# Chunk 0 of a delta-rule attention with an MLP: key scores first, query scores inside the substitution, w_in in its own row order

## The chip, the cores and the metric

The kernel runs on one core of a Trainium2 chip. The metric is the device time of one execution in microseconds; the time before is the median of three runs. Engines are named as in the profile: PE (matmuls; PEld are its weight loads), DVE, ACT, POOL, and SP, whose queue issues every DMA of this kernel.

## The reference

Two parts follow one another. The first is a delta-rule linear attention over B = 4 batches, H = 8 heads, S = 768 steps and D = 48; the second is an MLP with SiLU over 3072 rows, 384 wide, 2048 hidden.

```python
k_n = k / (np.linalg.norm(k, axis=-1, keepdims=True) + 1e-06)
state = np.zeros((B, H, D, D))
for t in range(S):
    kt, vt, bt = k_n[:, :, t], v[:, :, t], beta[:, :, t, None]
    y[:, :, t] = np.einsum('bhd,bhde->bhe', q[:, :, t], state)
    v_old = np.einsum('bhde,bhd->bhe', state, kt)
    state = state + bt[..., None] * np.einsum('bhd,bhe->bhde', kt, vt - v_old)
x = y.transpose(0, 2, 1, 3).reshape(B * S, H * D)
h = x @ w_in
out = (h * (1.0 / (1.0 + np.exp(-h)))) @ w_out
```

The weights come as 64-bit floats, so every piece of w_in and w_out is loaded raw (two words a number) and narrowed to 32 bits on the chip.

## The kernel before

**Chunks and units.** The 768 steps are cut into six chunks of 128; a unit is one batch in one chunk, with all eight heads. In a chunk, a triangular system is solved for each head: scores of keys with keys (j = 0) and of keys with queries (j = 1) are formed, the diagonal 32x32 blocks are inverted, and solve() combines them.

**Steps of a chunk.** squares() and norms() make the step sizes g (L338) from the keys alone. turn() transposes keys (its first part) and queries (its second) on PE (L376), and ACT copies them into kq (L383, L381). score() multiplies them (L399): with one weight load of the keys it takes keys and queries in one matmul of 256 columns, and ACT (L409) and DVE (L415) scale the results by g and mask them with `above` into ap. block_out() writes the diagonal blocks to DRAM by four DMAs a unit (L443), block_in() fetches them again as rows of g (L451), 32 partitions a unit. invert() is the substitution: 30 dependent steps on DVE, each a product (L477) and a sum (L481); at its end x goes out as up and its transposed copy g (ACT L485, DVE L486) as low (L492), and 12 DMAs move them into xe and xi (L502). solve() begins with merges (L551, four in all; first py, then px), goes on with seven steps k that pipeline inner, across, add, keep, old, update and new over the four units, and leaves the result in xT.

**The MLP.** feed_forward() multiplies xT by w_in (hidden(), L719), applies SiLU on ACT (L729), and multiplies by w_out (project(), L742, for chunk 0; combine(), L813, with fewer products, from chunk 1 on). It is a generator, `pieces`, that is advanced between the steps of the next chunk's preparation, substitution and solve, and so fills PE.

**Order.** pin() keeps the instructions of each compute engine in the order in which the program writes them; in_line() does the same for all DMAs on SP. Nothing overtakes on an engine. busy() is a dummy matmul (pw, L276; two instructions each) that keeps PE occupied where it has no work; one group of 20 of them stands before solve(0) and waits for a late step of the substitution.

**Weights.** w_in comes in eight pieces of 256 columns. Its rows are permuted (ROWS): partitions 0 to 47 and 64 to 111 hold the heads 0 to 5, and what is left of a 64-row half holds thirds of heads 6 and 7. So each piece is four DMAs (L215), over 48, 16, 48 and 16 partitions. narrow() takes three steps a piece: ACT L165 and L170, DVE L167, L173 and L177, and POOL L181. fill(n) advances n such steps. Pieces are kept in the spare places of other tiles until they are narrowed.

**From a unit's result to xT.** Rows of xT have the order of w_in's rows. In chunk 0, whose state is zero, a copy of heads 6 and 7 in thirds (`third`, L605) is used as weights by new() (L648), so that the sums come out in order, and one copy makes xT (L659). In the chunks 1 to 5 new() copies heads 6 and 7 to `last` (L662), the other six straight to xT (L665, on ACT and DVE), and six DMAs of 16 rows move the thirds (L669). load_q() for the next chunk follows on SP (L128).

Loads before the first score: beta, k of four units, q of four units, and two pieces of w_in.

Of the kernel before, what the change touches and what calls it, by code (L numbers as in the profile page):

```python
# [21 lines left out]
def kernel(  # L22
# [22 lines left out]
    nc = tc.nc  # L45
# [97 lines left out]
    for load_one in (load_k, load_q):  # L143
        for i in range(B):
            load_one(i)
    w_in = const.tile([P, NKT, DFF], FP32, name="w_in")
    HFF = NFF // 2


    ROWS = [  # L150
        (at, lambda a, e=e, n=n: (2 * a + e) * D if n == D else (6 + e) * D + a * (W - D), n)
        for e in range(2)
        for at, n in ((W * e, D), (W * e + D, W - D))
    ]
# [44 lines left out]
    def fetch_w_in(i):  # L199
# [7 lines left out]
        for at, row, rows in ROWS:  # L207
            step = row(1) - row(0)
            src = moe_w_in[row(0) : row(0) + rows, i * WF : (i + 1) * WF].bitcast(U32)
            pitch = src.ap[0][0]  # L210
            src = bass.AP(
                tensor=src.tensor, offset=src.offset,
                ap=[[pitch, rows], [pitch * step, NKT], [1, 2 * WF]],
            )
            in_line(nc.sync.dma_start(out=raw[at : at + rows], in_=src))  # L215
        raws[i] = raw.rearrange("p a (f j) -> p a f j", j=2)
# [7 lines left out]
    sums_of_w = [const.tile([P, NFF // 2, HM], FP32, name=f"sums_of_w{i}") for i in range(3)]  # L224

    def narrow_w_in(i):
        return narrow(w_in[:, :, i * WF : (i + 1) * WF], raws.pop(i))
# [3 lines left out]
    def fetch_w_out(i):  # L231
        if i in (0, 1, 5):
            raw = room(1, min(i, 1))
        elif i in (4, 7):
            raw = sums_of_w[2 if i == 4 else 0][:].rearrange("p f m -> p (f m)").bitcast(U32)
# [10 lines left out]
        raws[i] = raw.rearrange("p a (f j) -> p a f j", j=2)  # L246

    def narrow_w_out(i):
        at = 2 * i % HFF
        return narrow(w_outs[2 * i // HFF][:, at : at + 2, :], raws.pop(i))  # L250
# [45 lines left out]
    def squares(c):  # L296

        sums[c] = small.tile([P, BH], FP32, name="ss", bufs=1)[:]
        for b in range(B):
            if c == 1:  # L300
                sq = packed(zbufs[b])
            else:
                if b % HB == 0:
                    two = work.tile([P, HB, H, D], FP32, name="sq", tag="xg"[b // HB], bufs=1)
# [121 lines left out]

    def block_out(i, u):
# [19 lines left out]
    def block_in(i):  # L447
        b, c = units[i]
        there, g, _ = blocks[c]
        rows = slice(T * b, T * (b + 1))  # L450
        in_line(nc.sync.dma_start(out=g[rows], in_=there[b].rearrange("h j s t -> (h j) s t")))  # L451

    def invert(c):
# [41 lines left out]
        if c == 0:  # L495
            xe = sums_of_w[1][:].rearrange("p f m -> p (f m)")[:, 0 : BH * T]
# [16 lines left out]
    xTs, xes = {}, {}  # L513

    def solve(c, us):
# [6 lines left out]
        pzs, pys, third = {}, {}, {}  # L522
# [5 lines left out]

# [372 lines left out]
    for t in turning:  # L901
        next(t)
# [188 lines left out]
```

## Time and profile before

| what | value |
|---|---|
| median of 3 runs | 772.79 us (772.77 to 773.8) |
| the profiled execution, its own time | 770.21 us |
| its span | 768.5 us |
| mean granted clock | 0.977 |
| PE busy | 730.4 us (95%) |
| DVE busy | 411.8 us (54%) |
| ACT busy | 233.3 us (30%) |
| POOL busy | 83.6 us (11%) |
| moved by DMA | 50.93 MB in 155067 packets |

Times inside the profile are counted from the start of the span. A row of the timeline gives start, length, engine, line and operation, what is written and read, the shapes, how many, and in brackets the idle time before with what ended it. A row of the busy times by stretch gives the stretch, its length, the busy time of PE, PEld, DVE, ACT and POOL with the number of instructions, the granted share of the PE clock, the mean busy share of the DMA engines, and the GB/s that they moved. In the chain of waits a row is start, length and what the chain passed through; "issue" is time in which an engine waited for nothing that the profile shows.

### The profile page before, as it was taken

The page shows a single profiled execution, that of the slowest core. Times are in us where ns is not written, and L with a number is a line of the kernel's source. Part 1 is how long each engine was busy: PE and PEld are TensorE (multiplying, and loading weights), DVE is VectorE, ACT ScalarE, POOL GpSimd, SP SyncE. Part 2 cuts the span into 40 slices and gives each one's busy share as a digit, 9 for nine tenths or more (in the row PEclk, how much of TensorE's full clock was granted, in tenths as well). Part 3 has the DMA queues.
Part 4 walks back from the last instruction along what each step waited for, and adds up shares of the span by engine and source line. Part 5 has one row for each costly group of instructions (what it writes and reads, how often), then busy time and mean ns, then how long its engine had stood idle before and what let it go on. Part 6 is the DMA issues. An engine that isn't in the chain of part 4 may idle for free.

```text
span 768.5 us, 16585 instructions
## 1 busy us (share of the span) xinstructions
PE 730.4 (95%) x6806; PEld 630.0 (82%) x6806; DVE 411.8 (54%) x1050; ACT 233.3 (30%) x512; POOL 83.6 (11%) x95
## 2 busy tenths in 40 slices
PE   7549799899999999999999999999999999999997
PEld 5336587478777999997999997999998999999987
DVE  4886678892336672445672445672445682221212
ACT  4524465311325212315212315212315212312020
POOL 4005246300003000002000002000002000000000
PEclk8859999999999999999999999999999999999999
DMA  9798847212025213034113044113043013010000
GB/s 164 116 167 162 172 146 194 52 66 42 13 54 106 42 48 70 6 77 101 33 49 69 5 77 96 38 49 70 5 77 77 15 49 70 5 30 0 21 1 21
DMA packets 155067, 50.93 MB, mean 66 GB/s; under 512 B 142544, under 2 KB 147536, under 8 KB 154992
## 3 DMA queue, kind: packets, MB, share of 16 engines
q1 hardware_dynamic: 154992, 49.87, 31.1%
q8 instruction: 54, 0.88, 0.5%
q14 instruction: 21, 0.17, 0.1%
HBM read 34.70 MB, written 14.16 MB: 64 GB/s over the span
## 4 chain that ended last, share of the span: by engine, by line
PE 88%; DVE 4%; DMA 3%; SPq 2%; issue 1%; ACT 1%; POOL 1%; ACTq 0%; DVEq 0%
PE phid L719 31%; PE px L813 14%; PE py L813 11%; PE pa L399 6%; PE pz L583 4%; PE pt L376 3%; PE po L742 3%; PE pw L276 3%; PE pyc L642 3%; PE pyc L614 2%; PE ph L567 2%; DMA z<-in_q_dram 2%; PE px L551 2%; PE py L551 2%; PE pu L625 2%; DVE x L481 1%
## 5 line engine op out<-in xcount | busy, mean ns | idle before, releaser
L719 PE MATMUL phid<-xT,w_in 128*128 128x256 f32 x1152 | 260.7, 382 | 2.2 <-ACT gT L729 1.6
L719 PEld LDWEIGHTS phid<-xT,w_in 128*128 128x128 f32 x1152 | 214.8, 190 | 37.2 <-issue 6.3
L729 ACT ACTIVATE gT<-phid 128x512 f32<-128x512 f32 x96 | 57.3, 598 | 189.6 <-PE phid L719 149.2
L415 DVE SCALAR_TENSOR_TENSOR ap<-pa,g,above 128x128 f32<-128x128 f32 x192 | 58.2, 376 | 43.7 <-ACT ap L409 43.7
L481 DVE TENSOR_TENSOR x<-x,rank 128x30 f32<-128x30 f32 (+9 forms) x180 | 59.6, 331 | 7.4 <-ACT x L470 1.1
L477 DVE TENSOR_TENSOR rank<-g,x 128x30 f32<-128x30 f32 (+9 forms) x180 | 59.4, 330 | 5.0
L795 DVE TENSOR_TENSOR sums_of_g<-gT 128x384 f32<-128x384 f32 (+1 forms) x60 | 29.2, 509 | 57.9 <-ACT gT L729 47.3
L813 PE MATMUL py<-w_out,sums_of_g 128*128 128x192 f32 x320 | 56.8, 329 | 0.0
L813 PE MATMUL px<-sums_of_w,sums_of_g 128*128 128x192 f32 x320 | 56.8, 329 | 0.0
L813 PEld LDWEIGHTS px<-sums_of_w,sums_of_g 128*128 128x128 f32 x320 | 52.2, 190 | 1.4 <-issue 1.4
L813 PEld LDWEIGHTS py<-w_out,sums_of_g 128*128 128x128 f32 x320 | 52.2, 190 | 0.4
L409 ACT ACTIVATE ap<-pa,g 128x128 f32<-128x128 f32 x144 | 41.6, 365 | 32.2 <-PE pa L399 32.2
L399 PE MATMUL pa<-kq 48*128 48x256 f32 x384 | 51.0, 401 | 0.2 <-DVE ap L415 0.2
L742 PE MATMUL po<-w_out,gT 128*128 128x384 f32 x128 | 44.7, 495 | 2.9 <-POOL w_out L181 2.9
L399 PEld LDWEIGHTS pa<-kq 48*128 48x128 f32 x384 | 36.9, 192 | 12.1 <-issue 8.1
L583 PEld LDWEIGHTS pz<-vf,xi 64*64 64x64 f32 x768 | 37.3, 138 | 8.5 <-issue 7.3
L583 PE MATMUL pz<-vf,xi 64*64 64x48 f32 x768 | 41.8, 224 | 0.4 <-ACT raw L170 0.3
L601 ACT COPY z<-pz 64x384 f32<-64x384 f32 x48 | 22.7, 474 | 60.8 <-PE pz L583 54.7
L438 POOL MEMSET x<- 128x1024 f32 x6 | 5.7, 950 | 313.5 <-PE pz L583 251.2
L574 DVE TENSOR_TENSOR vf<-vf,ph 128x384 f32<-128x384 f32 x20 | 11.1, 554 | 53.2 <-PE ph L567 53.2
L742 PEld LDWEIGHTS po<-w_out,gT 128*128 128x128 f32 x128 | 23.3, 190 | 18.4 <-POOL w_out L181 4.2
L574 DVE TENSOR_TENSOR vf<-vf,pz 64x384 f32<-64x384 f32 x24 | 13.4, 557 | 42.8 <-PE pz L591 26.0
(132 smaller groups left out, 924.1 us busy)
## 6 DMA issues: line engine op xcount, KB each, us to landing
kb<-in_k_dram SPq DMA_DIRECT2D x24, 192.0 KB, 3.1
z<-in_q_dram SPq DMA_DIRECT2D x24, 192.0 KB, 3.5
vf<-in_v_dram SPq DMA_DIRECT2D x24, 192.0 KB, 3.9
out_dram<-o SPq DMA_DIRECT2D x24, 192.0 KB, 2.0
blocks<-ap SPq DMA_DIRECT2D x96, 32.0 KB, 1.7
g<-blocks SPq DMA_DIRECT2D x24, 128.0 KB, 2.5
up<-x SPq DMA_DIRECT2D x6, 512.0 KB, 2.6
low<-g SPq DMA_DIRECT2D x6, 512.0 KB, 2.9
```

Of the source, the lines that this page charges most:

```text
L399: u["last"] = pin(nc.tensor.matmul(pa[e][:, pp * 2 * C : (pp + 1) * 2 * C], lhsT=kq[rows, 2 * g + pp, 0, :], rhs=kq[rows, 2 * g + pp, :, : ...
L409: copied = pin(nc.scalar.activation(out=ap[:, h, 0, :], in_=pa[e][:, at : at + C], func=ACTF.Copy, scale=bt[:, h : h + 1],))
L415: masked = pin(nc.vector.scalar_tensor_tensor(out=ap[:, h, j:2, :], in0=pa[e][:, at + j * C : at + 2 * C].rearrange("p (j t) -> p j t", j= ...
L477: pin(nc.vector.tensor_tensor(out=tv, in0=g[:, 0:m, m : m + 1].to_broadcast([P, m, n]), in1=x[:, m : m + 1, m + 1 : T].to_broadcast([P, m, ...
L481: yield pin(nc.vector.tensor_tensor(out=x[:, 0:m, m + 1 : T], in0=x[:, 0:m, m + 1 : T], in1=tv, op=ALU.add))
L551: pin(nc.tensor.matmul(pm[to, at : at + T], lhsT=left, rhs=right, start=True, stop=True))
L583: yield pin(nc.tensor.matmul(pzs[x][rows, h, :], lhsT=xis[x // HB][rows, x % HB * H + h, :], rhs=vs[x][rows, h, :], start=True, stop=True,))
L719: pin(nc.tensor.matmul(ph[:, j * GT : (j + 1) * GT], lhsT=w_in[:, a, (2 * f + j) * P : (2 * f + j + 1) * P], rhs=xTs[c, hf][:, a, :], star ...
L729: pin(nc.scalar.activation(out=gTs[f // FG][:, f % FG, :], in_=ph[:], func=ACTF.Silu, scale=0.5))
L742: pin(nc.tensor.matmul(po[:, 0:DM], lhsT=gTs[f // 2 // FG][:, f // 2 % FG, at : at + C], rhs=w_outs[f // HFF][:, f % HFF, :], start=(f == ...
L795: pin(nc.vector.tensor_tensor(out=sums_of_g[:, k, fs], in0=of[0], in1=of[1], op=op))
L813: pin(nc.tensor.matmul(to, lhsT=at, rhs=quarter(f, *b) if isinstance(b, tuple) else sums_of_w[b][:, f], start=start and f == 0, stop=f == ...
```

## The change

Chunk 0: score_part() makes the key scores (j = 0) of all four units first, from keys alone; block_out and block_in follow, the latter for two units at once; only then come the loads of q. The second parts of the four turns and the query scores (j = 1) are written between the steps 5, 7, 9 and 11 of the substitution: matmul on PE, scaling on ACT, and the mask as a tensor_tensor on POOL. The loads of w_in's pieces 2 and 3, of the next q and of v are placed at its steps 4, 8 and 12; the key turns of chunk 1 at 14, 17, 20 and 23; the query turns of chunk 1 behind the substitution, with 9 dummy matmuls instead of 20. squares(1) and norms(1) come after three narrowing steps instead of before. In solve(0), four dummy matmuls instead of three stand in the first two steps.

Rows of w_in in natural order: each piece is one DMA over 128 partitions. For chunk 0, a `slab` with gaps holds copies of heads 1, 2, 5 and 6 so that new() can use weights shifted by any offset; keep's second copy takes four heads (192 elements) instead of two (96). For the chunks 1 to 5 new() copies everything to `part` (two copies of 128x256) and ten DMAs, one for each run of a head within a 128-row block, move it to xT. The scratch tile of squares() from chunk 2 on has the tag "g" for both halves, since `part` takes the tag "x".

```diff
-    for load_one in (load_k, load_q):
-        for i in range(B):
-            load_one(i)
+    for i in range(B):
+        load_k(i)
...
-        for at, row, rows in ROWS:
...
-            in_line(nc.sync.dma_start(out=raw[at : at + rows], in_=src))
+        src = moe_w_in.rearrange("(a p) f -> p a f", p=P)[:, :, i * WF : (i + 1) * WF].bitcast(U32)
+        in_line(nc.sync.dma_start(out=raw, in_=src))
...
-                    two = work.tile([P, HB, H, D], FP32, name="sq", tag="xg"[b // HB], bufs=1)
+                    two = work.tile([P, HB, H, D], FP32, name="sq", tag="g" if c > 0 else "xg"[b // HB], bufs=1)
...
+    def score_part(i, u, j, room):
+        b, c = units[i]
+        kq, bt = u["kq"], steps[c][:, b * H : (b + 1) * H]
+        if j == 0:
+            u["ap"] = work.tile([P, H, 2, C], FP32, name="ap", tag="ap", bufs=4)
+        ap = u["ap"]
+        pa = [bank(*room, f"pa{e}") for e in range(2)]
+        for p in range(NP):
+            for e in range(2):
+                rows = slice(W * e, W * e + D)
+                pin(nc.tensor.matmul(
+                    pa[e][:, p * C : (p + 1) * C], lhsT=kq[rows, p, 0, :], rhs=kq[rows, p, j, :],
+                    start=True, stop=True,
+                ))
+        for e in range(2):
+            if j == 0 and (e == 1 or b == B - 1):
+                pin(nc.vector.tensor_tensor(
+                    out=ap[:].rearrange("p (a e) j t -> p a e j t", e=2)[:, :, e, 0, :],
+                    in0=pa[e][:].rearrange("p (a t) -> p a t", a=NP),
+                    in1=bt.rearrange("p (a e) -> p a e", e=2)[:, :, e].unsqueeze(2).to_broadcast([P, NP, C]),
+                    op=ALU.mult,
+                ))
+                continue
+            for p in range(NP):
+                h = 2 * p + e
+                pin(nc.scalar.activation(
+                    out=ap[:, h, j, :], in_=pa[e][:, p * C : (p + 1) * C], func=ACTF.Copy,
+                    scale=bt[:, h : h + 1],
+                ))
+        if j == 1:
+            pin(nc.gpsimd.tensor_tensor(
+                out=ap[:, :, 1, :], in0=ap[:, :, 1, :],
+                in1=above[:].unsqueeze(1).to_broadcast([P, H, C]), op=ALU.mult,
+            ))
...
-            last = work.tile([P, C], FP32, name="last")
-            pin(nc.scalar.copy(last[:], pys[x][:, NKT * C : NP * C]))
...
+            if x == 0:
+                parts[c] = work.tile([P, 2, NP * C], FP32, name="part", tag="x", bufs=1)
+            part = parts[c][:, x % 2]
+            for n, engine in enumerate((nc.scalar.copy, nc.vector.tensor_copy)):
+                cols = slice(n * HB * C, (n + 1) * HB * C)
+                pin(engine(part[:, cols], pys[x][:, cols]))
+            for h in range(H):
+                f = D * h
+                while f < D * (h + 1):
+                    n, at = min(D * (h + 1) - f, P - f % P), W * (h % 2) + f - D * h
                     in_line(nc.sync.dma_start(
-                        out=xT[W * e + D : W * (e + 1), a, half],
-                        in_=last[W * e + n * a : W * e + n * (a + 1), :],
+                        out=xT[f % P : f % P + n, f // P, half],
+                        in_=part[at : at + n, C * (h // 2) : C * (h // 2 + 1)],
                     ))
+                    f += n
             load_q((c + 1) * B + x)
...
+    ORDER, SECOND = {4: (2,), 8: (3,), 12: ("q", "v")}, (5, 7, 9, 11)
+    TURN, REST = (14, 17, 20, 23), (4, 5, 6, 7)
...
-    turning = [turn(b, M, M) for b in range(2)]
+    turning = [turn(b, M, CC) for b in range(B)]
     us = [next(t) for t in turning]
     beta_of(0)
-    for t in turning:
-        next(t)
     norms(0)
     for b in range(B):
-        if b >= 1 and b + 1 < B:
-            us.append(list(turn(b + 1, M, M))[0])
-        go(score(b, us[b], (CC, A)), 3)
+        score_part(b, us[b], 0, (A, CC, M, A)[b])
         block_out(b, us[b])
-        if b > 0:
-            block_in(b - 1)
-    block_in(B - 1)
+        if b == HB:
+            block_in(0, HB)
+    block_in(HB, HB)
+    for i in range(B):
+        load_q(i)
...
     for n, done in enumerate(invert(0)):
...
-        if n in (3, 5, 7, 9):
-            next_us.append(list(turn(B + len(next_us), M, M))[0])
+        for of in ORDER.get(n, ()):
...
+        if n in SECOND:
+            b = SECOND.index(n)
+            next(turning[b])
+            score_part(b, us[b], 1, (A, CC)[b % 2])
+        if n in TURN:
+            turning.append(turn(B + len(next_us), M, M))
+            next_us.append(next(turning[-1]))
         if n == 18:
-            for i in range(20):
-                busy(done if i == 0 else None, Sync)
-    for i in range(4, NWI):
+            late = done
+    for t in turning[B:]:
+        next(t)
+    for i in range(9):
+        busy(late if i == 0 else None, Sync)
+    for i in REST:
         fetch_w_in(i)
...
     fill(3)
+    squares(1)
+    norms(1)
+    for i in (0, 1, 4):
+        more(i, ("in", 1))
...
-        for _ in range((3, 3, 2, 2, 1, 1, 1)[n] if n < 7 else 0):
+        for _ in range((4, 4, 2, 2, 1, 1, 1)[n] if n < 7 else 0):
             busy()
```

## The prediction

> **What bounds the kernel now.** I read the page first, then busy time by stages, then the chain of waits and the timeline where PE is not full. The page:
>
> ```profile
> PE 730.4 (95%) x6806; PEld 630.0 (82%) x6806; DVE 411.8 (54%) x1050; ACT 233.3 (30%) x512; POOL 83.6 (11%) x95
> ```
>
> PE is the bound, but not in every stage. Busy time by stretches (PE, PEld, DVE, ACT, POOL, granted clock, DMA share, GB/s):
>
> ```profile
> 33.50:56.00 22.50, 8.54 (x38) 6.70 (x39) 20.18 (x64) 5.88 (x15) 0.00 (x0) 0.53 1.22 166
> 56.00:68.00 12.00, 12.00 (x40) 6.82 (x40) 8.95 (x23) 4.47 (x7) 3.95 (x4) 1.00 0.65 155
> 68.00:98.70 30.70, 25.49 (x540) 18.44 (x539) 19.87 (x27) 15.82 (x30) 11.86 (x8) 0.94 0.87 182
> ...
> 182.00:768.00 586.00, 582.60 (x5661) 522.95 (x5659) 278.20 (x740) 154.38 (x352) 30.67 (x40) 1.00 0.20 45
> ...
> 40.00:45.00 5.00, 0.00 (x0) 0.00 (x0) 4.61 (x12) 0.00 (x0) 0.00 (x0) 0.50 1.06 175
> ...
> 115.00:119.00 4.00, 4.00 (x25) 3.27 (x25) 3.62 (x10) 2.18 (x3) 0.00 (x0) 1.00 1.03 415
> ```
>
> From 182 us on PE idles 3.4 of 586 us: little can be won there, much can be lost. Before 98.7 us PE has no real work to fill itself with; there the end is set by a serial path: loads, norms, scores, block_out/block_in, the substitution on DVE (33.5 to 56), its moves, then solve(0). During the substitution POOL does nothing at all (0.00). The chain of waits of that stretch, and the timeline:
>
> ```profile
> 55.12 12.90 PE pw L276 x40
> 68.03 1.13 PE py L551 x64
> 69.16 2.13 PE pw L276 x6
> ...
> 80.65 3.02 issue
> ...
> 98.67 1.35 PE phid L719 x5
> ```
>
> ```profile
> 33.55 0.36 DVE L468 COPY x<-g 128x16 f32<-128x16 f32 x3 [1.81 <-DMA g<-blocks]
> ...
> 55.98 0.61 DVE L486 COPY g<-x 128x512 f32<-128x512 f32 x1
> ...
> 233.78 0.83 POOL L352 TENSOR_TENSOR bkb<-kb,g 128x384 f32<-128x384 f32 x1
> 233.91 1.52 DVE L776 TENSOR_TENSOR w_out<-w_out 128x768 f32<-128x768 f32 x1
> 234.57 1.54 POOL L360 TENSOR_TENSOR vf<-vf,n 128x384 f32<-128x384 f32 x1
> ```
>
> The first merge (py L551) starts at 68.03 only because the 20 warm-up matmuls (pw) ahead of it end then: its own input, the first half of xe, was issued at 60.37 to 61.2 and lands about 2.5 us later (the median of those moves), at 63.3. So 4.7 us of slack lie in front of it. The last three rows matter most for what follows: a DVE tensor_tensor with both inputs in SBUF, 0.95 us in the undisturbed L776 rows (169 to 173 us), takes 1.52 beside a POOL tensor_tensor, and the next POOL one takes 1.54 instead of 0.83. They take turns.
>
> **Scores of the keys first: substitution earlier.** The chain g of the norms ends at 13.0 (last row of L338) and is not touched: it starts from k, not q. Key turns: four copies of 0.55 to 0.6 on ACT after the squares (8.8), so 11.2. Per unit 8 matmuls of 128 columns: at half clock L399 needs 3.72 us for 8 matmuls of 256 columns, so 1.86 a unit: done 12.7, 14.6, 16.4, 18.0. Then 4 ACT copies (0.88 for three, so 1.2) beside one DVE op (like L385's 128x512 PSUM copy, 0.68): ready 14.3, 15.9, 17.7, 19.4. SP issues four block_out DMAs in 1.8; block_in must wait 1.67 for landing: out0 to out2 end at 19.8, block_in(0,2), out3 ends 21.95, last block_in at about 24.0, landed 2.3 later. Substitution starts at 26.3 instead of 33.5: **-7.2** (error 1). The five narrowing steps on DVE (5.0 us in the old trace, from 26.8 to 31.7) now fit between 19.4 and 24.3.
>
> **Query scores inside the substitution: the mask on POOL.** Queries load behind block_in: q0 lands at about 27.3 (3.3 us, as kb at 31.31), the others 1.2 apart. Per unit PE turns and scores in 3.0 at half clock, ACT does 0.6 + 8 x 0.29 = 2.95; both are idle there now, so free. But the masks, formerly part of L415 on DVE, become four POOL tensor_tensors of 128x1024, at about 32, 35, 39 and 42, all between 26.3 and its end, where DVE runs 60 two-SBUF-input tensor_tensors back to back. POOL rows: 0.79 start to start for 384 elements (L352, x4 in 3.19), 1.85 for 768 (L181): by the first 2.1, by the second 2.5 for 1024. Lower bound 0 (they find gaps), upper 4 x 2.5 = 10. I take 4 x 2.2 = **+8.8**, since the row nearest to it (L776) shows the whole remaining time waited. The substitution then ends at 26.3 + 22.4 + 8.8 = 57.5 against 55.9: **+1.6**. The Trainium skill, "SBUF — State Buffer", section "SBUF: two separate sides", calls GpSimd's shared port pair with DVE an exclusive lock that also holds for DVE operations with two SBUF inputs; it speaks against this change, and by it the sum below is the same, while without it the first rival's holds.
>
> **Queries of chunk 1 behind the substitution; 20 warm-up matmuls become 9.** These four turns and copies now follow the substitution's last ACT copy (L485, 1.10), in ACT's order: 57.5 + 1.1 = 58.6, copies of 0.6; PE's third and fourth turns wait for banks and run 59.35 to 61.5 at half clock. Then 9 pw, 0.645 each warm, 1.29 cold. The granted clock was 0.5 from 32 to 54 and 0.84 between 54 and 56, so PE went warm about 5.7 us after its turns restarted at 48.9; so here warm at 62.8 to 66.2, pw done at 67.3 to 70.2. I take 68.8: first merge **+0.8** (xe is there at 57.5 + 7.3 = 64.8). So the shorter filler is eaten by the turns that were moved behind the substitution. Next, 4 pw instead of 3 after each of the first two merges, straight on the chain (three take 2.13 at 69.16): 2 x 0.71 = **+1.4**. keep's second copy has 192 elements instead of 96: 0.23 becomes about 0.31, two a step over four steps on the chain: **+0.6**. The count of matmuls in new(), 12 a unit, stays; the memset grows from 1536 to 1600 elements on an idle POOL; the queue of pieces is narrowed in the same order.
>
> **The 3.02 us "issue" wait** at 80.65 is PE waiting for nothing but its own instructions, and costs a cold clock behind it (0.5 between 86 and 88, 0.84 and 0.8 beside it; about 0.9 us). Four units add 8 matmuls each and 9 pw go, so it may move, shrink or stay: 0 to -3.9. I keep it.
>
> **w_in in natural order.** One 128-partition transfer per piece instead of four of 48 and 16. 175 GB/s in the stretch that only loads w_in, 415 in the one that loads w_out over 128 partitions: a piece takes 1.9 to 4.5 us instead of 4.5, and SP saves 24 issues of 0.43. On time: the raw pieces do not end the chain of 68 to 98.7 (PE, ACT and the 3.02 do), so 0. It covers something, though: ahead of up and low now stand q, k, w_in 2 and 3, q, v (4 x 0.8 + 1.6 MB); at the old 170 GB/s from 24.5 that is 52.5, still before 57.5. The Trainium skill, same page, section "Door 1: The DMA port swizzle", puts partitions 0 to 63 on half of the ports, 196 against 328 GB/s at 1 MiB; by it a piece would take 2.4 us as an estimate, and the sum stays the same.
>
> **Chunks 1 to 5: x in natural order.** Per unit two copies of 128x256 replace 128x128 and two of 48x384: ACT 0.27 + 0.47 becomes about 0.4, DVE 0.56 about 0.42: slightly less. DMAs: 10 instead of 6, at 0.63 start to start (L669), +2.5 a unit. From SP's start at 437.7 the four units end at 465 instead of 457; q is still in time (q2 lands at 462, its turn is at 469.3), x's readers too (units 0 and 1 land at 452.5, phid begins at 458.55). Behind them stand v, out and block_out: the first block_out slips from 464.3 to 470, but PE's pace of 5.6 a unit lets SP catch up to +1.7 at the fourth. The next merge has 3.6 us of slack (xe landed 412.7, merge 416.3). So 0; without that cover +1.7 a chunk. POOL's memset of x now waits for part's DMAs (436 to 466) with bkb and vf behind it, needed 20 us later. The squares' second half waits for the first's reduces, 0.7 on ACT, covered by PE's 1.4 us of px.
>
> **Sum.** 0.8 + 1.4 + 0.6 = +2.8. What is late at 98.67 stays late, PE being full from there (its 4.5 us of gaps from 142 to 171 come from POOL's w_out adds and ACT's L485, in the same order after). The profiled execution took 770.21 (1.7 around the span of 768.5), 2.6 below the median of 772.79; the difference is carried over: **775.6**.
>
> **Rivals.**
> *The masks cost nothing* (0.15). Against it the three rows; for it that no tensor_tensor of the substitution is ever beside POOL in this trace. Then the end is at 48.7, the first merge at 60.0 (-8.0), with +2.0 behind it -6: 766.8, and 763 without the issue wait. It decides when fewer than about 1.5 of the four masks are waited for.
> *The issue wait goes* (0.25): 2.8 - 3.9 = -1.1: 771.7, give or take 1.5.
> *SP falls behind in chunks 1 to 4* (0.12): if a 48-row DMA costs 0.9 instead of 0.63, SP's lag passes the 3.6 slack, 1 to 2.5 us in each of four chunks: 780 to 786.
> *As summed* (0.48): 775.6, give or take 1.8 (the warm-up's phase 1.5, mask 2.1 to 2.5).
>
> **Numbers.** 0.2% is 1.55 us, about what a measurement can tell here (runs spread 1.03). Faster: 0.15 + 0.10 of the second rival = 0.25. Same: 0.15 of it and 0.11 of the sum's lower edge = 0.26. Slower: 0.37 + 0.12 = 0.49. The range takes in the sum, the second rival, the upper half of the first and the lower edge of the third: 766.5 to 780.
>
> **What would show it.** Right: L468 at about 26; in the substitution several tensor_tensors of 2 us and more, each beside a POOL op; its end at 57; first py at 69; phid at 101.5; chunk period unchanged at 115.4. Wrong: undisturbed L477/L481 rows beside POOL; phid below 97; PE waits on xT or z after 182.

## The result: 3% slower

The changed kernel takes 796.42 us (median of 4, 792.5 to 796.97) against 772.78 us for the kernel before on the same chip: ratio 1.03, 95% interval 1.0259 to 1.0342. That is above the predicted range (766.5 to 780). The profiled execution took 796.97 us with a span of 795.0 us, 26.5 us longer than that of before (768.5), at a mean granted clock of 0.961 against 0.977.

The page's line for PE, to be read against the one of before: PE has only 46 more instructions, but 6.7 us more busy time and a longer span, so neither its work nor its pace is what it was.

```profile
PE 737.1 (93%) x6852; PEld 638.0 (80%) x6852; DVE 413.5 (52%) x1023; ACT 231.8 (29%) x512; POOL 92.4 (12%) x99
```

Busy time by stretches (columns as in the prediction). The first three rows answer to those of before; the fourth is the long stretch in which PE idled 3.4 us, and now idles 15.9; the last four are where it does so.

```profile
33.50:56.00 22.50, 14.36 (x92) 11.24 (x90) 21.33 (x35) 12.21 (x39) 9.69 (x4) 0.61 0.91 168
56.00:68.00 12.00, 6.26 (x21) 4.44 (x22) 7.89 (x18) 6.60 (x11) 6.35 (x6) 0.72 0.37 112
68.00:98.70 30.70, 28.30 (x554) 20.10 (x553) 27.35 (x48) 17.18 (x31) 9.52 (x6) 1.00 0.72 227
182.00:768.00 586.00, 570.09 (x5526) 509.37 (x5525) 269.18 (x727) 145.68 (x327) 29.68 (x40) 0.98 0.22 49
...
258.00:300.00 42.00, 37.38 (x189) 35.10 (x188) 26.80 (x79) 6.72 (x13) 0.00 (x0) 0.92 0.19 53
...
380.00:420.00 40.00, 37.03 (x192) 34.66 (x191) 26.61 (x79) 6.73 (x13) 0.00 (x0) 0.96 0.18 52
...
500.00:540.00 40.00, 35.07 (x182) 32.97 (x181) 26.70 (x79) 6.20 (x12) 0.00 (x0) 0.91 0.19 56
...
620.00:660.00 40.00, 36.97 (x186) 34.76 (x185) 26.88 (x79) 6.23 (x12) 0.00 (x0) 0.91 0.12 35
```

In each of these four stretches PE of before was busy throughout at clock 1.00. Here 4.62, 2.97, 4.93 and 3.03 us are missing, 15.55 in all, and the clock is 0.91 to 0.96, as it is 0.50 for a while behind each gap (262.53 to 269.36, 385.41 to 388.82, 504.88 to 511.70 and 627.76 to 634.58 us). In these four spells PE is busy for 5.61 + 3.41 + 4.10 + 6.05 = 19.2 us, of which half, 9.6, is lost against a full clock. The starts of the first px merge of a solve show it place by place: in the chunks 1 to 5 they are at 193.14, 305.83, 421.23, 536.62 and 652.02 in before, and at 192.51, 312.82, 433.26, 555.93 and 677.82 here, so PE is 0.6 us ahead, then 7.0, 12.0, 19.3 and 25.8 us behind. The four places cost 26.4 of the 26.5 us, one in each of the chunks 2 to 5, and some 25 of that are the gaps and the half clock behind them. Chunk 0 ends about where it did: the first phid is 0.96 us early (97.71 against 98.67).

The waits of PE from 182 us on say who ended the idle time:

```profile
PE px L857 <- ACT gT L773: 15.5, 4, 4.9
```

Why ACT is late is seen at the second place, around 382 us. SP's queue first (start, length, line, how many), then ACT, then PE, all of the changed kernel; last, the fourth block and ACT's copies in the kernel before:

```profile
329.60 6.92 SPq L712 DMA_DIRECT2D xT<-part  x10
...
337.25 7.23 SPq L712 DMA_DIRECT2D xT<-part  x10
...
345.20 6.23 SPq L712 DMA_DIRECT2D xT<-part  x10
...
352.16 6.48 SPq L712 DMA_DIRECT2D xT<-part  x10
...
360.26 3.35 SPq L133 DMA_DIRECT2D vf<-in_v_dram  x4
363.70 1.31 SPq L901 DMA_DIRECT2D out_dram<-o  x2
365.13 1.92 SPq L466 DMA_DIRECT2D blocks<-ap  x4
...
378.06 2.01 SPq L466 DMA_DIRECT2D blocks<-ap  x4
381.44 0.31 SPq L474 DMA_DIRECT2D g<-blocks  x1
```

```profile
377.14 0.60 ACT L773 ACTIVATE gT<-phid 128x512 f32<-128x512 f32 x1 [1.99 <-PE phid L763]
384.09 0.61 ACT L495 COPY x<-g 128x128 f32<-128x128 f32 x2 [6.36 <-DMA g<-blocks]
384.61 1.08 ACT L773 ACTIVATE gT<-phid 128x512 f32<-128x512 f32 x2
```

```profile
385.25 4.55 PE L857 MATMUL px<-w_out,gT 128*128 128x192 f32 x16 [2.97 <-ACT gT L773]
389.64 2.76 PE L857 MATMUL px<-sums_of_w,gT 128*128 128x192 f32 x16
```

```profile
365.62 1.78 SPq L443 DMA_DIRECT2D blocks<-ap  x4
368.67 0.31 SPq L451 DMA_DIRECT2D g<-blocks  x1
...
371.50 0.66 ACT L470 COPY x<-g 128x128 f32<-128x128 f32 x2 [0.89 <-DMA g<-blocks]
```

Four units of ten transfers keep SP busy without a pause until v, out and the blocks' turn comes. The last block goes out at 378.06 and the last block_in is issued at 381.44. On ACT, the substitution's first copies (L495) stand ahead of two gT activations whose input has long been there; the copies wait 6.36 us for the blocks, and PE, which needs those gT, stops for 2.97 us. Its next 16 matmuls take 4.55 us where the group behind takes 2.76: they run at half clock (0.50 from 385.41 to 388.82). In the kernel before, the four block_outs of this chunk started at 348.85, 354.44, 360.04 and 365.62, that is, SP waited for PE's pace of 5.6 us a unit, and the same copies waited 0.89 us.

### The profile page after: what moved, and what is told of

The parts are those of the page before. It is cut to its first block, busy times and chain, and to the rows that moved or that the text cites. A ratio compares the mean times of both kernels' runs of the same rounds, so it can differ in the third digit from the quotient of the medians.

```text
span 795.0 us, 16651 instructions
## 1 busy us (share of the span) xinstructions
PE 737.1 (93%) x6852; PEld 638.0 (80%) x6852; DVE 413.5 (52%) x1023; ACT 231.8 (29%) x512; POOL 92.4 (12%) x99
## 4 chain that ended last, share of the span: by engine, by line
PE 58%; DMA 4%; SPq 3%; POOL 1%; ACT 1%; issue 1%; DVE 0%; ACTq 0%; DVEq 0%
PE phid L763 19%; PE px L857 14%; PE py L857 10%; PE pz L609 3%; DMA blocks<-ap 2%; PE pa L386 2%; PE ph L593 2%; PE pyc L669 2%; PE pyc L641 2%; SPq L466 2%; PE py L577 1%; PE px L577 1%; PE pt L363 1%; PE pu L652 1%; DMA kb<-in_k_dram 1%; PE pz L617 1%
## 5 line engine op out<-in xcount | busy, mean ns | idle before, releaser
L506 DVE TENSOR_TENSOR x<-x,rank 128x30 f32<-128x30 f32 (+9 forms) x180 | 66.1, 367 | 7.4 <-ACT x L495 1.1
L402 DVE SCALAR_TENSOR_TENSOR ap<-pa,g,above 128x128 f32<-128x128 f32 (+1 forms) x160 | 48.5, 376 | 40.2 <-ACT ap L396 40.1
L502 DVE TENSOR_TENSOR rank<-g,x 128x30 f32<-128x30 f32 (+9 forms) x180 | 61.5, 342 | 5.0
L857 PE MATMUL px<-w_out,gT 128*128 128x192 f32 x160 | 38.0, 401 | 15.5 <-ACT gT L773 15.5
L857 PEld LDWEIGHTS px<-w_out,gT 128*128 128x128 f32 x160 | 34.6, 240 | 17.6 <-ACT gT L773 17.2
L396 ACT ACTIVATE ap<-pa,g 128x128 f32<-128x128 f32 x120 | 34.6, 365 | 28.6 <-PE pa L386 28.6
L386 PE MATMUL pa<-kq 48*128 48x256 f32 x320 | 40.9, 390 | 0.0
L600 DVE TENSOR_TENSOR vf<-vf,ph 128x384 f32<-128x384 f32 x20 | 11.1, 555 | 53.1 <-PE ph L593 53.1
```

The lines of the kernel that those rows point to most:

```text
L386: u["last"] = pin(nc.tensor.matmul(pa[e][:, pp * 2 * C : (pp + 1) * 2 * C], lhsT=kq[rows, 2 * g + pp, 0, :], rhs=kq[rows, 2 * g + pp, :, : ...
L396: copied = pin(nc.scalar.activation(out=ap[:, h, 0, :], in_=pa[e][:, at : at + C], func=ACTF.Copy, scale=bt[:, h : h + 1],))
L402: masked = pin(nc.vector.scalar_tensor_tensor(out=ap[:, h, j:2, :], in0=pa[e][:, at + j * C : at + 2 * C].rearrange("p (j t) -> p j t", j= ...
L502: pin(nc.vector.tensor_tensor(out=tv, in0=g[:, 0:m, m : m + 1].to_broadcast([P, m, n]), in1=x[:, m : m + 1, m + 1 : T].to_broadcast([P, m, ...
L506: yield pin(nc.vector.tensor_tensor(out=x[:, 0:m, m + 1 : T], in0=x[:, 0:m, m + 1 : T], in1=tv, op=ALU.add))
L857: pin(nc.tensor.matmul(to, lhsT=at, rhs=quarter(f, *b) if isinstance(b, tuple) else sums_of_w[b][:, f], start=start and f == 0, stop=f == ...
```

## Experiments

The theories: **T1**, SP is late because of ten transfers a unit, and the waiters behind it are those just shown; **T2**, the tile `part`, which shares its room with x, holds POOL's memset back (the waits show POOL waiting 433 us for part's transfers); **T3**, the new order of chunk 0 shifts the later chunks. Theories on chunk 0 (W, M) came up on the way. All results first; each ratio is to the kernel before on the same chip, with its 95% interval, and phid is the start of the first phid in the profiled run. One profile of phid says little by itself: kernels with the same chunk 0 have it at 92.3 to 96.8 (old order, one transfer, `slab`) and at 97.4 to 101.3 (new order). c_win and l_order_win read w_in in natural order against features in the old one, so their product is another.

| label | order of chunk 0 | w_in, transfers a piece | xT transfers a unit on SP | median us | ratio | phid |
|---|---|---|---|---|---|---|
| before | old | 4 | 6 | 771.5 to 772.8 | 1 | 98.7 |
| after | new | 1 | 10 | 796.42 | 1.0300 (1.0259 to 1.0342) | 97.7 |
| a_order | new | 4 | 6 | 779.2 | 1.0094 (1.0062 to 1.0127) | 107.7 |
| b_rows | old | 1 | 10 | 785.85 | 1.0198 (1.0154 to 1.0243) | 94.1 |
| d_four | old | 4 | 6 + 4 idle | 788.46 | 1.0220 (1.0184 to 1.0256) | 99.7 |
| f_dve | new | 1 | 10 | 794.8 | 1.0313 (1.0267 to 1.0359) | 101.3 |
| c_win | old | 1 | 6 | 765.23 | 0.9918 (0.9884 to 0.9951) | 92.3 |
| h_v | new | 1 | 10 | 787.84 | 1.0206 (1.0145 to 1.0267) | 99.9 |
| e_late | new | 1 | 10 | 791.86 | 1.0261 (1.0193 to 1.0329) | 97.6 |
| i_best | old | 1 | 10 | 778.1 | 1.0071 (1.0043 to 1.0099) | 96.8 |
| e_late2 | new, masks late | 1 | 10 | 786.55 | 1.0174 (1.0125 to 1.0223) | 95.0 |
| l_order_win | new | 1 | 6 | 772.05 | 0.9998 (0.9974 to 1.0023) | 97.8 |
| j_scalar | old | 1 | 8 | 767.23 | 0.9952 (0.9912 to 0.9992) | 95.1 |
| j_gpsimd | old | 1 | 8 | 765.51 | 0.9918 (0.9884 to 0.9952) | 92.3 |
| n_after_pool | new | 1 | 8 | 773.2 | 1.0012 (0.9991 to 1.0034) | 97.4 |
| m_best | new, masks late | 1 | 8 | 769.22 | 0.9966 (0.9942 to 0.9991) | 95.1 |

**a_order: the new order alone.** Chunk 0 as in after; ROWS, `third`, `last` and the six transfers as in before.

```diff
-        src = moe_w_in.rearrange("(a p) f -> p a f", p=P)[...].bitcast(U32)
-        in_line(nc.sync.dma_start(out=raw, in_=src))
+        for at, row, rows in ROWS:
+            ...
+            in_line(nc.sync.dma_start(out=raw[at : at + rows], in_=src))
...
-                        in_=part[at : at + n, C * (h // 2) : C * (h // 2 + 1)],
+                        in_=last[W * e + n * a : W * e + n * (a + 1), :],
```

> The new order of chunk 0 alone; rows of w_in and the way of x into the feed-forward as in before. Theory T1 (SP is late): ten transfers a unit instead of six keep SP from the block transfers of the next chunk, ScalarE waits for them in the first copies of the substitution with the gT activations behind it, and TensorE stops for 3 to 5 us and then runs at half clock, four times. Here there are six transfers again: no TensorE gap over 1.5 us behind 180 us, the first phid at 97.7, and the span some 1 us under that of before: 767.5, a time of about 769.2 to 772. T2 (the tile `part`, which shares its room with x, holds the POOL memset back) expects the same. T3 (the new order of chunk 0 shifts the later chunks against SP) expects the four gaps to stay, 790 to 797.

Measured: no PE gap over 0.7 us behind 182 us, as T1 and T2 said and T3 did not. But the time, 779.2, is what none of them expected: the new order costs 7 us by itself (9 between the two profiled runs), all before the first phid, which starts at 107.7, 9.0 later than in before. There the substitution starts at 30.7 and its up goes out at 61.6, the first merge is at 72.6, and further on PE stands still again for reasons of its own (timeline of PE):

```profile
94.58 0.24 PE L619 MATMUL pz<-vf,xi 64*64 64x48 f32 x1 [4.23 <-issue]
```

So the "issue" wait has not gone; it has grown to 4.23 us, with half clock behind it (0.62 from 95 to 105 us). That the changed kernel ends chunk 0 in time must come from the other half of the change.

**b_rows: the rows alone.** The old order; w_in, slab, part and ten transfers of after.

```diff
-            for e in range(2):
-                for a in range(NKT):
-                    in_line(nc.sync.dma_start(out=xT[W * e + D : W * (e + 1), a, half], in_=last[...]))
+            for h in range(H):
+                f = D * h
+                while f < D * (h + 1):
+                    ...
+                    in_line(nc.sync.dma_start(out=xT[f % P : f % P + n, f // P, half], in_=part[...]))
```

> The natural rows of w_in alone, with the ten transfers a unit and the tile `part`; the order of chunk 0 as in before. T1 and T2: the four TensorE gaps are there, 13 to 17 us together, with half clock behind each; the first phid at 98.7 as in before; time about 26 us over before, 796 to 799. T3: no gaps, 771 to 774.

Measured: the waits of px for gT are there (12.3 us, four times, of 6.5, 2.5, 3.0 and 0.3 us), and the loss with them; T3 has fallen. The time is under the expected 796 to 799, in part because the gaps are fewer, in part because the first phid is at 94.1, not 98.7: in this profile the rows bring 4.6 us in chunk 0 before they lose four times that.

**d_four: four idle transfers on SP.** Before, with rows, order and tiles untouched.

```diff
+            for n in range(4):
+                in_line(nc.sync.dma_start(
+                    out=last[W * (n // 2) + 3 * 16 : W * (n // 2 + 1), 64 * (n % 2) : 64 * (n % 2 + 1)],
+                    in_=last[W * (n // 2) : W * (n // 2) + 16, 64 * (n % 2) : 64 * (n % 2 + 1)],
+                ))
             load_q((c + 1) * B + x)
```

> Before, with four more transfers a unit on SP, from `last` into rows of `last` that nobody reads (idle work); rows, order and tiles as in before. T1: four transfers at 0.59 to 0.63 us are 2.5 us a unit, so the gaps appear at the same four places, 10 to 17 us together, and the time is 18 to 28 us over before (790 to 799). T2: it is not the count of transfers but the shared tile: within 1 us of before.

PE's rows with idle time behind 182 us, and SP's for one unit:

```profile
264.90 5.33 PE L818 MATMUL px<-w_out,gT 128*128 128x192 f32 x16 [4.38 <-ACT gT L734]
385.57 4.55 PE L818 MATMUL px<-w_out,gT 128*128 128x192 f32 x16 [2.54 <-ACT gT L734]
469.28 2.87 PE L818 MATMUL py<-w_out,sums_of_g 128*128 128x192 f32 x16 [1.69 <-DVE o L826]
506.60 2.87 PE L818 MATMUL px<-w_out,gT 128*128 128x192 f32 x16 [1.73 <-ACT gT L734]
```

```profile
330.19 3.68 SPq L669 DMA_DIRECT2D xT<-last  x6
333.91 2.48 SPq L674 DMA_DIRECT2D last<-last  x4
```

Four transfers of 16 rows are 2.48 us on SP, and they alone make the kernel before 2.2% slower, at the same places. T1 holds; T2 isn't needed, since `part` does not exist here. (The copies to `last` on ACT also wait for these transfers, 20.7 us in all; but in chunk 3 SP's queue has no pause of more than 0.5 us from 330.19 to the first block at 364.24, so it is SP's own time that makes the blocks late.) The cost is a little under the expected 18 to 28 us (788.46 against 771.51, 17 us); the place in chunk 5 is spared.

**f_dve: is it ACT's queue?** After, with the copies that waited in ACT's queue given to DVE from chunk 2 on.

```diff
-            if n < T // 4:
+            if n < T // 4 or c > 1:
                 done = pin(nc.vector.tensor_copy(out=squares_of(x), in_=squares_of(g)))
             else:
                 pin(nc.scalar.copy(squares_of(x), squares_of(g)))
```

> After, with the substitution's first copies on VectorE alone from chunk 2 on, so that ScalarE does not wait for the blocks. T1 with its second half (the waiter that matters is ScalarE, the gT activations being queued behind its copy): the TensorE gaps of 3 to 5 us fall below 1 us each although SP is as late as in after (last block_in of chunk 3 issued at about 381), and the time is 769 to 778. Rival R (late blocks hold TensorE anyway, through VectorE's sums or the merges): the gaps move behind but stay, 790 to 797.

Measured: 794.8, no better. The waits of px for gT are gone, but DVE now stands 11.1 us at its first copy (L493), and what is queued behind it, sums_of_g and o, holds PE instead:

```profile
PE py L857 <- DVE o L865: 11.3, 6, 2.7
PE px L857 <- DVE sums_of_g L839: 3.0, 3, 1.2
PE py L857 <- DVE sums_of_g L839: 1.5, 2, 1.3
```

So the second half of T1, as I had put it, was wrong: ACT is only the first of two in-order queues that hold work of the MLP behind the blocks. Relief has to come before the blocks, on SP.

**c_win: one transfer a piece, in before.** The first phid of b_rows, 94.1, raised the question whether w_in brings it.

```diff
-        for at, row, rows in ROWS:
-            ...
-            in_line(nc.sync.dma_start(out=raw[at : at + rows], in_=src))
+        src = moe_w_in.rearrange("(a p) f -> p a f", p=P)[:, :, i * WF : (i + 1) * WF].bitcast(U32)
+        in_line(nc.sync.dma_start(out=raw, in_=src))
```

> Before, with the pieces of w_in read in natural order, one transfer each instead of four, and nothing else: the features that meet them are still in the old order, so the product is another; every instruction but these transfers is that of before. Theory W (one transfer a piece frees SP and the DMA engines early in chunk 0; it is what moved the first phid of b_rows from 98.7 to 94.1): z transfers issued from about 35.7 instead of 40.3, the first merge at 62 to 63 instead of 68.0, no issue wait of 3 us, the first phid at 94 to 95; no gap behind 182 us; time 3 to 6 us under before. Rival (the gain of b_rows came from chunk 0's shorter way of x, slab and one copy): the first phid at 98 to 99, the time within 1.5 us of before.

W holds, and a little more than it said: 0.8% faster (6 to 7 us), first phid at 92.3. SP's queue and the first PE row that depends on it, in c_win and then in before:

```profile
34.77 1.50 SPq L208 DMA_DIRECT2D w_out<-in_moe_w_in_dram  x2
36.31 7.17 SPq L128 DMA_DIRECT2D z<-in_q_dram  x4
```

```profile
44.10 1.12 PE L369 MATMUL pt<-ident,z 128*128 128x128 f32 x4 [7.76 <-DMA z<-in_q_dram]
```

```profile
34.40 4.24 SPq L215 DMA_DIRECT2D w_out<-in_moe_w_in_dram  x8
40.34 7.92 SPq L128 DMA_DIRECT2D z<-in_q_dram  x4
...
48.92 1.12 PE L376 MATMUL pt<-ident,z 128*128 128x128 f32 x4 [13.14 <-DMA z<-in_q_dram]
```

In before, the two pieces were eight issues and 4.24 us, z began at 40.34, and PE's turns at 48.92 (after 13.14 us of waiting for z). The 20 warm-up matmuls stand behind those turns, and so the first merge: 62.95 instead of 67.96. An "issue" wait is still there, but of 1.9 us.

**h_v: v behind the blocks.** After, with v's four loads moved behind the last block_in in chunks 3 to 5, and its scaling (size) behind that; the loads of chunk 2 are issued by another line and stayed, though the expectation counts them in.

```diff
             load_k(i + B)
-            size(i)
+            if b == B - 1:
+                for n in range(c * B, (c + 1) * B):
+                    load_v(n)
+                for n in range(c * B, (c + 1) * B):
+                    size(n)
...
-            for n in range((c + 2) * B, (c + 3) * B):
-                load_v(n)
```

> After, with the four transfers of v (3.35 us on SP) and the scaling of v moved from ahead of the block transfers to behind the last of them, in chunks 2 to 5. T1 (SP is late): the blocks are out some 3.3 us earlier, so the gaps of 4.62, 2.97, 4.93 and 3.03 us fall to about 1.3, 0, 1.6 and 0, with less half clock behind them: 16 to 25 us under after, 771 to 780. Rival (the blocks are late for another reason, their way through DRAM or the POOL memset behind part's transfers): less than 5 us under after.

Measured: the gap of chunk 2, which was not touched, stays (4.52 us); the other three go from 2.97, 4.93 and 3.03 to 0, 1.03 and 0, as T1 said. But the time falls by 9 us only (787.84), half of what was expected: further on PE now waits 2.19, 2.70 and 1.78 us for o, as in f_dve. DVE's substitution still starts late, and POOL's scaling of v now runs beside it (products and sums of 0.27 to 0.30 us take up to 0.93). My reading, not tested further: SP's lateness has two waiters, and 3.3 us of relief serve only the first.

**i_best: the same in b_rows.** b_rows (old order, natural rows) with v behind the blocks as in h_v. Expected were 766 to 772, at or under before, with the first phid at 94 to 95 and the gaps of 6.5, 2.5 and 3.0 us down to about 3, 0 and 0. Measured: 778.1, 0.7% slower than before, so a miss. The gap of chunk 2, whose v stayed ahead of the blocks, is 5.74 us; the other two are gone, but PE waits 1.94 and 1.52 us for o instead, and the first phid is at 96.8.

**e_late: masks behind the substitution.**

```diff
-        if j == 1:
-            pin(nc.gpsimd.tensor_tensor(out=ap[:, :, 1, :], in0=ap[:, :, 1, :], in1=above..., op=ALU.mult))
...
+    for u in us:
+        pin(nc.gpsimd.tensor_tensor(out=u["ap"][:, :, 1, :], in0=u["ap"][:, :, 1, :], in1=above..., op=ALU.mult))
```

> After, with the four masks on POOL moved behind the substitution. The price of a mask beside the substitution is 2.0 to 2.2 us each by after's rows (L506 at 2.42 to 2.58 beside a mask, 0.41 without). Theory M (these are on the path): the substitution ends at 51.5 to 52.5 instead of 60.1, the first merge is at 61.5 to 63 instead of 69.9, the first phid 6 to 8 us earlier, and the four gaps stay: 787 to 791. Rival (the path of q and the warm-up matmuls ends as late): the substitution ends early but the first merge is at 67 or later, the time within 3 us of after.

The edit did nothing: written later, the masks still had nothing to wait for on POOL, and ran at 36.2 to 50.6, as in after (36.57 to 51.05). It tells neither M nor its rival apart. Its 791.86 against 796.42 is what two runs of one schedule can differ by (the intervals, 1.0193 to 1.0329 and 1.0259 to 1.0342, overlap); first phids of after, e_late, h_v and f_dve, whose chunk 0 is the same, are 97.6 to 101.3.

**e_late2: the masks made to wait.** e_late, with the first mask behind the last sum of the substitution:

```diff
...
+        if n == 0:
+            behind(mask, last, Sync)
```

> After, with the four masks made to wait for the last sum of the substitution (in e_late POOL had nothing ahead of them to wait for, and ran them at 36 to 53 us as before). Theory M: the four sums and products at 2.4 to 2.6 us take 0.4 again, so the substitution ends at 51 to 52.5 instead of 60.1, the first merge is at 61 to 63.5 instead of 69.9, the first phid at 90 to 94 instead of 97.6 to 101.3; the four gaps of chunks 2 to 5 stay; 785 to 790. Rival (q, warm-up matmuls or transfers end as late): the first merge at 67 or later, the time within 3 us of after.

DVE's end of the substitution in e_late2, and in after the four operations that ran beside a mask:

```profile
51.21 0.19 DVE L501 TENSOR_TENSOR x<-x,rank 128x30 f32<-128x30 f32 x1
51.44 0.61 DVE L506 COPY g<-x 128x512 f32<-128x512 f32 x1
```

```profile
36.81 2.42 DVE L506 TENSOR_TENSOR x<-x,rank 128x220 f32<-128x220 f32 x1
41.44 2.57 DVE L506 TENSOR_TENSOR x<-x,rank 128x238 f32<-128x238 f32 x1
46.26 2.58 DVE L506 TENSOR_TENSOR x<-x,rank 128x238 f32<-128x238 f32 x1
51.46 2.42 DVE L502 TENSOR_TENSOR rank<-g,x 128x210 f32<-128x210 f32 x1
```

M holds for the substitution: it ends 8.7 us earlier (60.10 against 51.44), and the first merge is at 62.3 instead of 69.9. Of these 7.7 us only 2.7 arrive at the first phid (95.0, where 90 to 94 was expected): PE waits 1.9 us for DVE's sum of v and pz, which stands behind narrowing steps of w_in on DVE, and its clock is 0.50 from 82.7 to 89.5 us. The masks are now 10.1 us in a row on POOL, with its narrowing behind them; that they cause this wait is likely, but not shown. The four gaps stay, but shorter (4.73, 1.79, 2.82 and 1.38 us), which makes up most of the gain; the time is 786.55.

**l_order_win: the order with quick w_in.** a_order with the edit of c_win.

> The new order of chunk 0 alone (a_order) with w_in's pieces read as in c_win (one transfer each, natural rows against features in the old order, so the product is another). It sets the order's price free of the w_in transfers: by the first phid of the kernels with one transfer a piece, 92.3, 94.1 and 96.8 in the old order and 97.6, 97.7, 99.9 and 101.3 in the new, some 4.7 us. So the first phid at 97 to 101, no gap behind 182 us, and 768 to 773, some 5 us over c_win. Rival (the order costs nothing once w_in is one transfer, a_order's 9 us being the issue wait and the clock alone): 763 to 767.

As expected: 772.05, no gap, phid 97.8. Between c_win and l_order_win lies the order's price, 0.8% or 6 us (the intervals do not touch); between a_order and l_order_win the gain of w_in under the new order, 1%. The two add up: 1.0094 times 0.9918 is 1.001, and 0.9998 was measured.

**j_scalar and j_gpsimd: xT transfers on another queue.** b_rows with the transfers of h below HB issued by ACT, or by POOL.

```diff
-                    in_line(nc.sync.dma_start(out=xT[...], in_=part[...]))
+                    if h < HB:
+                        pin(nc.gpsimd.dma_start(**to))
+                    else:
+                        in_line(nc.sync.dma_start(**to))
```

> b_rows (old order of chunk 0, natural rows) with five of a unit's ten xT transfers issued by ScalarE's queue instead of SP's. T1 (SP's time is what makes the blocks late): SP has five transfers a unit, fewer than before's six, so the blocks are as early as in before and the gaps go; ScalarE pays some 0.6 us for each, 3 us a unit, in idle time; the first phid at 94 to 97; 762 to 769, under before. Rival (ScalarE's issue time holds gT up, or the way of x is late anyway): gaps of 1 to 3 us at each of the 16 units or so, 775 to 790.

> The same with POOL's queue in place of ScalarE's for the five transfers. T1: POOL is idle for most of chunks 1 to 5, so the gaps go and the time is 762 to 769. Rival (POOL's issues are dearer than SP's, or its memset and masks stand behind them): PE waits for xT, 775 to 790.

HB is 2, so that two of the ten were moved and not five, as I had written. Even so no gap over 0.5 us is left in either, and both are faster than before. The transfers of j_gpsimd (shortest, median and longest ns, then first and last start):

```profile
L684 SPq DMA_DIRECT2D xT<-part x160: 514/587/1824, 203.2 to 683.5; - x160
L682 POOL DMA_DIRECT2D xT<-part x40: 502/502/700, 203.5 to 676.3; - x40
```

```profile
346.80 1.84 SPq L431 DMA_DIRECT2D blocks<-ap  x4
...
350.91 3.40 SPq L431 DMA_DIRECT2D blocks<-ap  x4
...
361.02 2.02 SPq L431 DMA_DIRECT2D blocks<-ap  x4
```

Two transfers less a unit are 1.2 us a unit on SP, some 5 us over four units, and the last block goes out at 361.0 in place of 374.8 in b_rows (whose chunk 3 also starts later by the stall of chunk 2). Between eight a unit and ten lie 20 us: the slack ends between them.

**n_after_pool and m_best.** The same two transfers on POOL in after, and in e_late2.

> After, with two of a unit's ten xT transfers issued by POOL instead of SP (h below HB, which is below 2; the two runs before this one, j_scalar and j_gpsimd, also moved two of ten and not five, as was written for them). T1: eight a unit on SP were enough in the old order, so the gaps go here too; what is left is the new order's price, as in l_order_win: 768 to 775, within 0.4% of before. Rival (the new order itself makes the blocks late as well): gaps stay at two places or more, 780 to 790.

> The same with the masks made to wait for the substitution, as in e_late2 (first phid 95.0, against 92.3 to 96.8 in the old order with one transfer a piece). If the masks are the whole price of the order and the keys' scores first bring nothing else: as j_gpsimd, 763 to 768. If the earlier substitution pays once nothing else is in its way: 757 to 762. If the order has a price besides the masks: 768 to 773.

n_after_pool: 773.2, ratio 1.0012, one gap of 1.6 us left. So the late blocks were 22 to 23 us of the changed kernel's 24 (1.0300 to 1.0012), in place, and what remains is the order's price and w_in's gain, which cancel. m_best: 769.22, in the third expectation: the order has a price besides the masks. Without the masks' lock the order is still no better than the old one (j_gpsimd 765.5), though by the intervals, 0.9942 to 0.9991 and 0.9884 to 0.9952, the two barely differ. Where the rest of the order's price goes wasn't tried; PE's wait for DVE's sum of v and pz (1.9 us) and a clock of 0.81 between 85 and 95 us in m_best are there to see. The version that beats both kernels is j_gpsimd: the old order, natural rows, two transfers a unit on POOL.

## Why the prediction was wrong

**The step that failed: "Chunks 1 to 5: x in natural order", "So 0".** First its size. Four units on SP were to end 8 us later; in chunk 4, which the step worked with, they take 30.3 us (450.04 to 480.34) instead of 19.3, 11 more, since ten transfers take 6.25 to 7.26 us and not 6.3. Counted against PE's own last score matmul of the chunk (2.7 us ahead of the fourth block_out in every chunk of before: 362.94 and 365.62 in chunk 3, here 370.05 and 378.06), the first block_out is 8.9 us late in chunk 4 where the sum had 5.7, and 9.2 in chunk 3. From there SP catches up by 0.5 (chunk 4) to 1.4 us a unit, where the step had 1.3: a unit's blocks mostly take SP 4 to 5 us (four block_outs in 2.0, the wait for their landing, block_in and k) against PE's 5.6. At the fourth, 1.7 us was to be left; it is 6.9, 5.3, 7.3 and 5.6 in the chunks 2 to 5.

Then its cover. The slack named was the 3.6 us of the next merge; the first to wait is the substitution's first copy, and in ACT's queue gT stands behind it. The gaps (4.62, 2.97, 4.93 and 3.03) are 2.3 to 2.6 us shorter than the lags: so much this path covers. A lag of 1.7 would have cost nothing here too: in j_gpsimd it is 0 to 2.2 us, with no gap. n_after_pool prices the step at 22 to 23 us (796.4 to 773.2) instead of 0, the half clock behind the gaps being some 10 of it, which the prediction had nowhere.

**Rival "SP falls behind in chunks 1 to 4"** (0.12) had the right place and sign. Its condition, 0.9 us a transfer, wasn't met (0.59 median) and wasn't needed; its price, 1 to 2.5 us a chunk, was 5.0 to 7.6 with the clock.

**"w_in in natural order": 0, measured 6 to 7 us of gain.** The step said that the raw pieces don't end the chain. They do not, but two of them stand on SP ahead of z, and z decides when PE turns, when the warm-up matmuls end and when the first merge starts. I had read that the 20 matmuls end late, and not asked what they had waited for; PE's row at 48.92 had said it, 13.14 us for z. The slack of 4.7 us in front of the merge was about the size of the gain to be had. The 175 GB/s of 40 to 45 us, read as w_in alone, had q's loads in it too (issued from 40.34). How long one piece takes by itself no run shows: beside other loads the first four land 6.6 us after their issue in after.

**The order: +2.8, measured 6 to 7.** Right: a mask costs a whole wait of 2.0 to 2.2 us (8.4 in all, 8.8 predicted), as the lock that was cited has it, which refutes the first rival. Off: the substitution starts at 29.2 and not 26.3, as the last block_in is issued at 25.6 (24.0 predicted) and takes some 3.5 us to land in place of 2.3; with w_in as before, at 30.7. Its end, 60.1 (57.5 predicted), and the first merge, 69.9 (68.8), follow from that. The issue wait was kept in the sum; it grew in a_order and was absent in after. So the order cost some 4 us more than summed and w_in brought 6 to 7 that were put at 0, and the first phid of after fell 0.96 us ahead of before where the sum had it 2.8 behind. That the sum is off there by less than 4 us is luck: it was made of two terms wrong by 4 to 7 us in opposite ways. Two slips in the working changed nothing: 0.6 + 8 x 0.29 is 2.92 and not 2.95, and nine dummy matmuls from 61.5 with the clock full at 62.8 end at 68.0 and not 67.3.

**The signs that were named** told the cases apart in part: the long sums beside POOL were there; of the signs for "wrong", PE's waits behind 182 us came true, though for gT and not for xT.

## What to carry to other kernels

Ahead of a transfer that slips on a queue without gaps, look for its first waiter on every engine, and then at what stands behind that waiter in the same queue: an engine that is 30% busy stops a full PE through one copy at its head. Count what a queue does per unit against the pace of the engine that it serves; when it is near, a few more small transfers cost nothing until the slack is gone (two more a unit here), and then 20 us (four more). Where filler work ends a chain, ask what the filler waited for.

## What the runs showed of the hardware

A PE gap costs more than its length. From 130 us on, behind gaps of 4.38 us and more, the next 16 matmuls always took 4.4 to 5.5 us instead of 2.8 (after, b_rows, d_four, e_late, e_late2, h_v, i_best); behind gaps up to 2.19 us they never did. Between, length doesn't decide: gaps of 2.70 us were followed by 4.3 to 5.5 us four times in f_dve, and by 2.87 in h_v. What decides is where the gap lies. The granted clock changes on a grid of 3.41 us: the half clock of after begins at 262.53, 385.41, 504.88 and 627.76, whole multiples of 3.41 us apart, and lasts 6.83, 3.41, 6.82 and 6.82 us. Take the stretches between two points of that grid in which the clock is full. From 130 us on, in all runs, each of these in which PE stood still for 2.02 us or more was followed by half clock (f_dve, 523.14 to 526.55: 2.02; after, 501.46 to 504.88: 2.2), and none with 1.95 us or less was (b_rows, 498.63 to 502.05: 1.95, the rest of its gap of 2.97 us lying in the next one). The Trainium skill, "TensorE: Matmul & The Clock Gate", section "Part 1: The HAM clock gate", has the clock fall after at least one idle window of about 3.4 us, and the window run freely. The free window agrees with the grid; but the window need not be idle throughout, 2.0 us of it were enough here, so far as the trace's modelled ends of matmuls can tell.

A transfer from SBUF to SBUF of 8 to 24 KB holds SP for 0.59 us (median), whatever its rows (16 in before, up to 48 in after), and POOL for 0.50 (j_gpsimd); eight transfers of 96 and 288 KB of w_in took SP 4.24 us in before where two of 768 KB took 1.50 in c_win.
